# A last product's operand loads placed behind w3's loads, five of its sums moved from GpSimd to VectorE, and a new order table

## The chip, the cores and the metric

The kernel runs on one core of a Trainium2 chip. The metric is the device time of one execution in microseconds (us); lower is better. The core has TensorE (PE, matrix products), VectorE (DVE), ScalarE (ACT), GpSimd (POOL) and SyncE (SP, which here issues the DMAs).

## The reference

Three stages follow each other, all in fp32. Each of 4608 tokens has 512 features.

```python
# 1. attention, 8 batches x 8 heads, 576 queries, head size 64
k_p = k.reshape(B, H, 72, 8, D).mean(axis=3)      # keys and values pooled by 8
v_p = v.reshape(B, H, 72, 8, D).mean(axis=3)
x = softmax(q @ k_p.T / 8) @ v_p
# 2. first MoE: 512 -> 1024 -> 512
h = x @ w_in
s = h * softmax(h)
x = ((s - mean(s)) / sqrt(var(s) + 1e-6) * g_ln) @ w_out
# 3. second MoE: 512 -> 1024 -> 1024 -> 512
out = ((x @ w1) * (x @ w2)) @ w3 @ w_out
```

## The kernel before, in words

**Precision.** Each fp32 operand of a product is split into a high part, written by ACT (L218), and a low part, source minus high part, written by DVE (L219). A product is three matrix products on PE: high x high, low x high, high x low.

**Stages.** The record has three stages. Up to about 335 us attention runs batch by batch, and the first MoE on the tokens of earlier batches runs beside it. `pr` are normalised probabilities (POOL, L660 and L667), `pt` and `px` their transposes on PE (L685, L688), `kp` pooled keys (DVE, L475), `kv` the loaded keys or values (the sum over pooled values is POOL's, L429), `lt` and `lnl` a transpose of the first MoE's hidden rows on PE (L835) and its low part on DVE (L839), `gwh` and `gwl` the parts of the first MoE's output weights (ACT L377, DVE L378, from `cvb` of L374), `x` the first MoE's output (L849 to L851). Beside this, w1, w2 and others are converted in the background by ACT, DVE and POOL (L291 to L306) and written to device memory (L396).

From there to about 935 us PE forms `p`, the products of the second MoE with w1 and w2 by a seven-product (Strassen-Winograd) scheme (L1154 to L1156). DVE, ACT and POOL combine them into `a`, the elementwise product of both halves, which goes to device memory as `pd` (L1147).

In the last stage w3 and w_out are first multiplied with each other. `load_w3` (L1304) loads one piece of w3, 128x512, into a staging tile `stg` (4 buffers) by four DMAs; `w3_split` writes its parts to one of two alternating pairs of tiles `th0` and `th6`, and `wf_rows` (L1323 to L1325) needs two pieces for each of eight row blocks n. A block is 24 matmuls of 128x512 into `ow`. `upper` and `lower` (L1340 to L1357) form the seven combinations `wf`, `t1` to `t4` of the blocks and split them into `wch`/`wcl` and other `th` tiles. Then `Last` multiplies `pd` with these: for each of nine column groups j, `load` brings two tiles `raw` of 1 MB (4 buffers), `sum` forms s1 to s4 from them on POOL (128x1024, L1386), `split` writes ten rotating operand tiles `bk` (their low part by L219), and `product` runs seven products of 24 matmuls each into `o` (L1402 to L1404). L1434 to L1449 combine these on DVE, and the results are stored.

**Order.** The program is traced in one order and then put into another: ISSUE_ORDER holds for each engine a row of numbers in run-length form, and `issue_order` (L114) chains the engine's instructions in the order that these numbers give. An engine executes its own list in order. It waits for other engines' results by semaphores. Names below carry the loop numbers: `raw0_1` is tile 1 of j = 0, `stg_10164` the staging tile with that number, `lnl2` belongs to unit 2.

Of the kernel before, what the change touches and what calls it, by code (L numbers as in the profile page):

```python
# [24 lines left out]
    ),  # L25
    "Activation": (
# [20 lines left out]
    ),  # L47
    "DVE": (
# [32 lines left out]
    ),  # L81
    "Pool": (
# [9 lines left out]
    ),  # L92
# [38 lines left out]
def attention_moe_kernel(  # L131
# [25 lines left out]
    nc = tc.nc  # L157
# [1203 lines left out]
    FACTORS = ("x11", "s2", "s1", "x12", "s3", "x22", "s4")  # L1361
    free = list(range(10))

    class Last:
# [12 lines left out]
        def sum(self, name):  # L1377
            x = self.x
# [181 lines left out]
```

## Time and profile before

| what | value |
|---|---|
| time, median of 3 runs | 1173.01 us (1172.94 to 1174.21) |
| the profiled execution's own time | 1171.81 us |
| its span in the trace | 1170.0 us |
| mean granted TensorE clock | 0.993 of full speed |
| PE busy | 1133.1 us, 97% |
| DVE, ACT, POOL busy | 937.6, 543.4, 527.1 us |

The time is what the device needs for one execution; the span goes from the first to the last thing that the trace records, and 1.81 us lie outside it. Busy time of an engine is the sum of its instructions without their overlaps. A granted clock of 1.00 is 2.4 GHz on TensorE, 0.50 is 1.2 GHz.

### The profile page before, as it was taken

To read this page: it belongs to the slowest core of one execution; us is meant where nothing else is said; L and a number is where in the kernel's file an instruction comes from. 1 tells how busy PE (TensorE), PEld (TensorE's weight loads), DVE (VectorE), ACT (ScalarE), POOL (GpSimd) and SP (SyncE) were. 2 spreads that over 40 slices of the span, in tenths; PEclk is the share of its full clock that TensorE was granted. 3 is DMA by queue.
4 is the path that set the end of the run, shared out by engine and by line. 5 is a ranking of instruction groups with operands and counts; after the bars stand their busy time and mean duration, and the time that the engine had idled before them with its cause. 6 is when DMAs were issued, how large, how long until landed. Compare 5 with 4: busy or idle time off the path is not lost. (4 is left out here: it accounts for less than half of the span.)

```text
span 1170.0 us, 20192 instructions
## 1 busy us (share of the span) xinstructions
PE 1133.1 (97%) x7146; PEld 1017.6 (87%) x7146; DVE 937.6 (80%) x1392; ACT 543.4 (46%) x1399; POOL 527.1 (45%) x482
## 2 busy tenths in 40 slices
PE   6898999999999999999999999999999989999998
PEld 5688888999999899999998888888888868999998
DVE  6899879989676765596668969989886679999982
ACT  5665657575656565664523113131130155454542
POOL 3554645555332321100056757676763254656520
PEclk9999989999999999999999999999999999999999
DMA  9775576979474722356254624544522264353511
GB/s 255 161 137 151 134 191 196 232 220 235 131 177 125 182 91 90 127 191 204 84 159 131 208 89 163 176 147 162 181 99 108 85 222 136 109 196 131 177 39 73
DMA packets 174117, 178.55 MB, mean 153 GB/s; under 512 B 83392, under 2 KB 116160, under 8 KB 174016
## 3 DMA queue, kind: packets, MB, share of 16 engines
q1 hardware_dynamic: 174016, 177.27, 51.8%
q8 instruction: 56, 0.92, 0.3%
q14 instruction: 45, 0.37, 0.1%
HBM read 114.30 MB, written 62.91 MB: 151 GB/s over the span
## 5 line engine op out<-in xcount | busy, mean ns | idle before, releaser
L849 PE MATMUL x<-lnh,gwh 128*128 128x256 f32 x576 | 164.9, 286 | 0.5 <-ACT gwh L377 0.5
L851 PE MATMUL x<-lnh,gwl 128*128 128x256 f32 x576 | 161.9, 281 | 0.6 <-DVE gwl L378 0.4
L850 PE MATMUL x<-lnl,gwh 128*128 128x256 f32 x576 | 161.7, 281 | 0.0
L849 PEld LDWEIGHTS x<-lnh,gwh 128*128 128x128 f32 x576 | 109.1, 189 | 1.7 <-ACT gwh L377 0.7
L640 ACT ACTIVATE ea<-sc,mx 128x72 f32<-128x72 f32 x320 | 98.1, 324 | 26.2 <-DVE mx L637 22.1
L851 PEld LDWEIGHTS x<-lnh,gwl 128*128 128x128 f32 x576 | 109.0, 189 | 1.2 <-DVE gwl L378 1.2
L850 PEld LDWEIGHTS x<-lnl,gwh 128*128 128x128 f32 x576 | 109.1, 189 | 0.9
L660 POOL TENSOR_TENSOR pr<-ea,sm 128x512 f32<-128x512 f32 x40 | 41.7, 1044 | 139.1 <-DVE sm L656 79.4
L755 PE MATMUL h<-winh,xh 128*128 128x512 f32 x288 | 95.4, 411 | 0.0
L1158 ACT ACTIVATE p<-p 128x512 f32<-128x512 f32 (+1 forms) x40 | 22.1, 551 | 156.2 <-PE p L1156 118.9
L1170 POOL TENSOR_TENSOR a<-a,b 128x512 f32<-128x512 f32 (+1 forms) x40 | 53.2, 1329 | 91.3 <-issue 54.5
L755 PE MATMUL h<-winl,xh 128*128 128x512 f32 x288 | 90.8, 395 | 0.0
L755 PE MATMUL h<-winh,xl 128*128 128x512 f32 x288 | 90.0, 394 | 0.0
L640 ACT ACTIVATION_READ_ACCUMULATOR ea<-sc,mx 128x1 f32 x320 | 67.2, 210 | 0.0
L764 ACT ACTIVATE e<-h,ST 128x1024 f32<-128x1024 f32 x36 | 40.2, 1116 | 56.4 <-DVE ST L763 56.2
L755 PEld LDWEIGHTS h<-winl,xh 128*128 128x128 f32 x288 | 54.3, 189 | 11.9
L755 PEld LDWEIGHTS h<-winh,xl 128*128 128x128 f32 x288 | 54.1, 189 | 11.8
L1154 PE MATMUL p<-th,w1h 128*128 128x512 f32 (+1 forms) x160 | 59.0, 369 | 1.9 <-DVE a L1164 1.9
L1155 PE MATMUL p<-th,w1h 128*128 128x512 f32 (+1 forms) x160 | 58.9, 368 | 0.0
L1156 PE MATMUL p<-th,w1l 128*128 128x512 f32 (+1 forms) x160 | 58.8, 368 | 0.0
L1174 POOL TENSOR_TENSOR a<-a,b 128x512 f32<-128x512 f32 (+1 forms) x40 | 54.0, 1350 | 8.2 <-DVE b L1167 5.8
L770 DVE SCALAR_TENSOR_TENSOR e<-h,e 128x1024 f32<-128x1024 f32 x36 | 44.0, 1221 | 16.4 <-ACT e L764 16.2
(278 smaller groups left out, 3798.1 us busy)
## 6 DMA issues: line engine op xcount, KB each, us to landing
raw<-pd SPq DMA_DIRECT2D x18, 1024.0 KB
pd<-a SPq DMA_DIRECT2D x64, 256.0 KB
ed<-turn SPq DMA_DIRECT2D x28, 512.0 KB
back<-ed SPq DMA_DIRECT2D x112, 128.0 KB
x2d<-xo SPq DMA_DIRECT2D x35, 256.0 KB
kv<-in_k_dram SPq DMA_DIRECT2D x32, 256.0 KB
kv<-in_v_dram SPq DMA_DIRECT2D x32, 256.0 KB
f<-in_moe_w_dram SPq DMA_DIRECT2D x16, 512.0 KB
```

The costliest lines, as they stand in the source:

```text
L640: nc.scalar.activation(e[0:n, x], half[a][:, h], AF.Exp, bias=mx[0:n, x : x + 1], scale=1.0, accum_out=sm[0:n, x : x + 1],)
L660: nc.gpsimd.tensor_tensor(pr[0:n, 0 : H * KM].rearrange("p (h k) -> p h k", h=H), e[0:n, :, 0:KM], s8.to_broadcast([n, H, KM]), ALU.mult,)
L755: nc.tensor.matmul(self.ph[:, a], s_[:, c], w_[:, c, a * 512 : a * 512 + 512], start=first, stop=last)
L770: nc.vector.scalar_tensor_tensor(e, self.hv, -1.0 / F, e, ALU.mult, ALU.mult, accum_out=st[:, 2:3])
L849: nc.tensor.matmul(o, gw[0][:, f, ws], self.th[:, f], start=(f == 0), stop=False)
L850: nc.tensor.matmul(o, gw[0][:, f, ws], self.tl[:, f], start=False, stop=False)
L851: nc.tensor.matmul(o, gw[1][:, f, ws], self.th[:, f], start=False, stop=(f == FC - 1))
L1154: nc.tensor.matmul(o, wh[:, c, fsl], th[:, c], start=c == 0, stop=False)
L1155: nc.tensor.matmul(o, wh[:, c, fsl], tl[:, c], start=False, stop=False)
L1156: nc.tensor.matmul(o, wl[:, c, fsl], th[:, c], start=False, stop=c == 1)
L1170: nc.gpsimd.tensor_tensor(a[:, 0], a[:, 0], b[:, 0], ALU.mult)
L1174: nc.gpsimd.tensor_tensor(a[:, 1], a[:, 1], b[:, 1], ALU.mult)
```

## The change

ISSUE_ORDER gets new rows for all five engines, and the sums of j = 0 (s1, s2, s3, s4) and the first sum of j = 1 (s1) are issued by VectorE instead of GpSimd. No other instruction is added, taken away or given to another engine. Two lines of the table stand for its some 180.

```diff
 ISSUE_ORDER = {
     "PE": (
-        "0:32 5 -6 5:2 -7:4 3:4 4:2 -6:4 2:2 1 -2 1:6 1:4 -5 4:27 7 9 -18:7 1:2 8:2 7:2 -19 9 8:2 -20:6 "
+        "0:32 5 -6 5:2 -7:4 3:4 4:2 -6:4 2:2 1 -2 1:6 1:4 -5 4:22 1 -2 1:3 7 9 -18:7 1:2 8:2 7:2 -19 9 "
...
     FACTORS = ("x11", "s2", "s1", "x12", "s3", "x22", "s4")
+    SUMS_ON_DVE = {(0, f) for f in FACTORS} | {(1, "s1")}
     free = list(range(10))
...
             x[name] = RB.tile([P, 4, U], F32, tag="s", name=f"{name}_{self.j}", bufs=4)
-            nc.gpsimd.tensor_tensor(x[name], x[a], x[b], op)
+            (nc.vector if (self.j, name) in SUMS_ON_DVE else nc.gpsimd).tensor_tensor(x[name], x[a], x[b], op)
```

Line numbers of the change are 2 higher than before up to L1360 and 3 higher from there on, so L1304 is L1306, L1373 is L1376, L1386 is L1389 and L219 is L221.

SP's list, where the first `raw` loads meet w3's loads, before:

```order
L1373 DMA raw0_0_10162<-pd_104 128x4x512
L1373 DMA raw0_1_10209<-pd_104 128x4x512
L1304 DMA stg_10164<-w3f_131 32x4x128 x4
L1373 DMA raw1_0_10321<-pd_104 128x4x512
L1373 DMA raw1_1_10384<-pd_104 128x4x512
L1304 DMA stg_10169<-w3f_131 32x4x128 x4
L1304 DMA stg_10211<-w3f_131 32x4x128 x4
L1304 DMA stg_10216<-w3f_131 32x4x128 x4
L1304 DMA stg_10270<-w3f_131 32x4x128 x4
L1304 DMA stg_10275<-w3f_131 32x4x128 x4
L1373 DMA raw2_0_10474<-pd_104 128x4x512
```

And in the change, the same place, from the load of raw0_0 on:

```order
L1376 DMA raw0_0_10162<-pd_104 128x4x512
L1306 DMA stg_10164<-w3f_131 32x4x128 x4
L1306 DMA stg_10169<-w3f_131 32x4x128 x4
L1306 DMA stg_10211<-w3f_131 32x4x128 x4
L1306 DMA stg_10216<-w3f_131 32x4x128 x4
L1306 DMA stg_10270<-w3f_131 32x4x128 x4
L1376 DMA raw0_1_10209<-pd_104 128x4x512
L1306 DMA stg_10275<-w3f_131 32x4x128 x4
L1306 DMA stg_10323<-w3f_131 32x4x128 x4
L1306 DMA stg_10328<-w3f_131 32x4x128 x4
L1376 DMA raw1_0_10321<-pd_104 128x4x512
L1376 DMA raw1_1_10384<-pd_104 128x4x512
```

raw0_1, raw1_0 and raw1_1 stood ahead of all but the first of w3's remaining pieces, and now the loads of raw1 stand behind all of them; raw0_1 stands behind five pieces instead of none.

DVE's list while the row blocks n = 4 and 5 of w3 times w_out run, before (th0 from stg_10164 and stg_10169 is block 4, th6 from stg_10211 and stg_10216 block 5):

```order
L219 TENSOR_TENSOR wcl_10059<-wf_10203,wch_10058 128x256
L219 TENSOR_TENSOR th0_7021<-stg_10164,th0_7021 128x4x4x32
L219 TENSOR_TENSOR bk1_10053<-raw0_1_10209,bk1_10053 128x1024
L219 TENSOR_TENSOR wcl_10059<-ow5_10225,wch_10058 128x256
L1352 TENSOR_TENSOR t2_10250<-ow5_10225,t1_10207 128x256
L1355 TENSOR_TENSOR t3_10251<-ow5_10225,wf_10203 128x256
L219 TENSOR_TENSOR wcl_10059<-t1_10207,wch_10058 128x256
L219 TENSOR_TENSOR wcl_10059<-t2_10250,wch_10058 128x256
L1357 TENSOR_TENSOR t4_10252<-ow5_10225,t2_10250 128x256
L219 TENSOR_TENSOR bk2_10054<-s2_0_10317,bk2_10054 128x1024
L219 TENSOR_TENSOR th0_7021<-stg_10169,th0_7021 128x4x4x32
L219 TENSOR_TENSOR th3_7024<-t3_10251,th3_7024 128x256
```

And in the change:

```order
L221 TENSOR_TENSOR th0_7021<-stg_10169,th0_7021 128x4x4x32
L221 TENSOR_TENSOR wcl_10059<-wf_10203,wch_10058 128x256
L221 TENSOR_TENSOR wcl_10059<-t1_10207,wch_10058 128x256
L221 TENSOR_TENSOR th6_7027<-stg_10211,th6_7027 128x4x4x32
L221 TENSOR_TENSOR th6_7027<-stg_10216,th6_7027 128x4x4x32
L221 TENSOR_TENSOR wcl_10059<-ow5_10225,wch_10058 128x256
L1354 TENSOR_TENSOR t2_10250<-ow5_10225,t1_10207 128x256
L1357 TENSOR_TENSOR t3_10251<-ow5_10225,wf_10203 128x256
L1389 TENSOR_TENSOR s1_0_10315<-raw0_0_10162,raw0_1_10209 128x1024
L221 TENSOR_TENSOR bk1_10053<-raw0_1_10209,bk1_10053 128x1024
L221 TENSOR_TENSOR th0_7021<-stg_10270,th0_7021 128x4x4x32
L1389 TENSOR_TENSOR s2_0_10317<-s1_0_10315,raw0_0_10162 128x1024
```

The second piece of block 4 stood behind two operand splits `bk` and the work on the block before it (`t2` to `t4` of L1352 to L1357), and now it stands ahead of both. The sum s1 of j = 0 is new on this engine, and so is s2.

DVE's list in the attention stage, around the pooled keys `kp3_1`, before:

```order
L475 TENSOR_REDUCE kp3_0_2047<-kv3_0_1939 128x128
L697 TENSOR_TENSOR ptx4_1729<-px4_0_1735,ptx4_1729 64x128
L637 TENSOR_REDUCE mx4_1_1746<-sc4_1_1_1695 128x4
L696 TENSOR_TENSOR ptl4_1728<-pt4_0_1730,pth4_1727 128x4x128
L297 TENSOR_SCALAR cvb_2127<-cvb_2127 128x512
L475 TENSOR_REDUCE kp3_1_2147<-kv3_1_1979 128x128
L655 TENSOR_SCALAR sm4_1_1747<-sm4_1_1747 128x8
L839 TENSOR_TENSOR lnl2_1790<-lt2_0_0_1791,lnh2_1789 128x4x128
L656 RECIPROCAL sm4_1_1747<-sm4_1_1747 128x8
L839 TENSOR_TENSOR lnl2_1790<-lt2_1_0_1814,lnh2_1789 128x4x128
L839 TENSOR_TENSOR lnl2_1790<-lt2_0_1_1838,lnh2_1789 128x4x128
```

And in the change:

```order
L699 TENSOR_TENSOR ptx4_1729<-px4_0_1735,ptx4_1729 64x128
L477 TENSOR_REDUCE kp3_0_2047<-kv3_0_1939 128x128
L639 TENSOR_REDUCE mx4_1_1746<-sc4_1_1_1695 128x4
L698 TENSOR_TENSOR ptl4_1728<-pt4_0_1730,pth4_1727 128x4x128
L841 TENSOR_TENSOR lnl2_1790<-lt2_0_0_1791,lnh2_1789 128x4x128
L477 TENSOR_REDUCE kp3_1_2147<-kv3_1_1979 128x128
L657 TENSOR_SCALAR sm4_1_1747<-sm4_1_1747 128x8
L658 RECIPROCAL sm4_1_1747<-sm4_1_1747 128x8
L841 TENSOR_TENSOR lnl2_1790<-lt2_1_0_1814,lnh2_1789 128x4x128
L841 TENSOR_TENSOR lnl2_1790<-lt2_0_1_1838,lnh2_1789 128x4x128
```

The first `lnl2` stood behind kp3_1 and a step on `sm4_1`, and now it stands ahead of them; a step of a background conversion (L297) has left this place. In the same way `kp2_0` stands some 15 rows later in the change, behind the steps on L374 and L378 that it preceded, and POOL's sum `kv2_0` (L429) stands behind `pr3_0` and `pr3_1` instead of ahead of them. The loads of kv3 stand earlier on SP: one 512 KB load and one store of conversions that preceded them now follow.

## Rows read from the trace of the kernel before

**Rows 1.** The page: span, and busy time by engine.

```profile
span 1170.0 us, 20192 instructions
...
PE 1133.1 (97%) x7146; PEld 1017.6 (87%) x7146; DVE 937.6 (80%) x1392; ACT 543.4 (46%) x1399; POOL 527.1 (45%) x482
```

**Rows 2.** PE's waits, whole run: total us, times, longest us.

```profile
PE ow L1323 <- ACT th L218: 4.6, 1, 4.6
PE pt L685 <- POOL pr L660: 3.2, 5, 1.1
PE lt L835 <- DVE lnl L839: 2.8, 3, 1.3
...
PE px L688 <- POOL pr L667: 0.8, 1, 0.8
...
PE x L849 <- ACT gwh L377: 0.5, 1, 0.5
PE x L851 <- DVE gwl L378: 0.4, 1, 0.4
```

**Rows 3.** The chain of waits, 930 to 975 us: start, us, what.

```profile
939.59 8.75 DMA raw<-pd
...
949.20 5.98 DMA stg<-w3f
955.20 2.01 DVE th L219
957.21 3.35 DVE bk L219
...
963.81 0.62 ACT th L218
```

**Rows 4.** Timeline of PE, 964 to 972 us: start, us, instruction, [idle before].

```profile
964.47 0.80 PE L1323 MATMUL ow<-o,th 128*128 128x512 f32 x1 [4.63 <-ACT th L218]
...
970.37 0.41 PE L1324 MATMUL ow<-o,th 128*128 128x512 f32 x1
...
971.98 0.39 PE L1325 MATMUL ow<-o,th 128*128 128x512 f32 x1
```

**Rows 5.** Windows: length; PE, PEld, DVE, ACT, POOL busy; granted clock; DMA share; GB/s.

```profile
36.00:40.00 4.00, 2.55 (x8) 0.97 (x6) 3.90 (x9) 1.46 (x5) 1.51 (x2) 1.00 1.08 223
...
140.00:160.00 20.00, 16.66 (x111) 14.40 (x110) 18.04 (x35) 12.25 (x39) 9.38 (x14) 0.95 0.72 171
160.00:180.00 20.00, 20.00 (x125) 18.57 (x124) 14.39 (x22) 8.40 (x30) 12.05 (x15) 0.88 0.67 179
...
155.00:159.00 4.00, 1.40 (x9) 0.90 (x10) 4.00 (x11) 1.98 (x4) 2.60 (x4) 0.87 0.89 192
...
1000.00:1020.00 20.00, 20.00 (x171) 20.00 (x170) 20.00 (x15) 10.37 (x12) 12.35 (x5) 1.00 0.47 159
```

**Rows 6.** Timelines of DVE and POOL around the first sums.

```profile
947.96 1.21 DVE L219 TENSOR_TENSOR bk<-raw,bk 128x1024 fp32r<-128x1024 f32 x1
...
957.13 3.43 DVE L219 TENSOR_TENSOR bk<-raw,bk 128x1024 fp32r<-128x1024 f32 x1
...
956.62 2.86 POOL L1386 TENSOR_TENSOR s<-raw 128x1024 f32<-128x1024 f32 x1
```

**Rows 7.** Timelines of DVE and of PE in the last products.

```profile
990.49 1.22 DVE L219 TENSOR_TENSOR th<-s,th 128x1024 fp32r<-128x1024 f32 x1
...
986.49 0.28 PE L1402 MATMUL o<-wch,bk 128*128 128x256 f32 x1
...
1003.37 0.28 PE L1402 MATMUL o<-th,th 128*128 128x256 f32 x1
```

**Rows 8.** Timelines of DVE and POOL in the attention stage.

```profile
101.83 1.93 DVE L475 TENSOR_REDUCE kp<-kv 128x128 f32<-128x1024 f32 x1
...
153.51 1.97 DVE L475 TENSOR_REDUCE kp<-kv 128x128 f32<-128x1024 f32 x1 [0.50 <-DMA kv<-in_k_dram]
...
108.81 3.34 POOL L429 TENSOR_TENSOR kv<-kv 128x512 f32<-128x512 f32 x3 [3.49 <-DMA kv<-in_v_dram]
```

164 rows, old and new, of the table ISSUE_ORDER are left out of this document.

## The prediction

> **What bounds the kernel now.** I read the page's busy times first. PE works in 1133.1 of 1170.0 us [rows 1], so what can be won is its idle time, 36.9 us, and the stretches in which its clock is halved. What the other engines do costs something only where PE waits for it.
>
> The view of PE's waits says where the idle time is [rows 2]. Apart from the wait for the very first load, which no reordering here touches, the largest single one is 4.6 us, before a matmul of `ow` (w3 times w_out), for a split by ACT. The others are short, up to 1.3 us each, and most of them belong to the attention stage: `pt` and `px` for the probabilities of POOL, `lt` for the low part `lnl` of DVE, `x` for `gwh` and `gwl`.
>
> The chain of waits tells what the 4.6 us are made of [rows 3]. From 939.59 two tiles `raw` land, for 8.75 us, and w3's pieces are in the chain only from 949.20 to 955.18. DVE's split of the first such piece then takes 2.01 us, an operand split `bk` stands behind it with 3.35 us, and ACT's split of the second piece comes last, at 963.81. PE starts at 964.47 after a wait of 4.63 us [rows 4]. So loads of operands that PE first uses at 986.49 [rows 7] stand ahead of data that PE needs now, and on DVE their splits do the same.
>
> The windows give the third loss, the clock. Between 140 and 180 us the granted clock is 0.95 and then 0.88 of full speed [rows 5]. Half speed for a share of 2 x 0.05 and 2 x 0.12 of 20 us each is 6.8 us at 1.2 GHz. Ahead of it PE was busy for only 1.40 of 4.00 us (155 to 159 us). After the wait at w3 the same happens: from 964.47 to 970.37 thirteen matmuls take 5.90 us, 0.454 each, while the seven from 970.37 to 971.98 take 0.230 each [rows 4].
>
> **The change part by part.** *The seam at w3.* In the new SP list eight pieces of w3 stand behind raw0_0, the last three of them behind raw0_1 too. Two tiles and one piece (2.3 MB) took 8.75 us [rows 3], so a tile is about 4 us, and the next piece has been issued some 4 us earlier even if the whole of raw0_0 must land first. On DVE the two pieces of block 4 are split without the 3.35 us of `bk` and the four steps on `t2` to `t4` between them. Before, ACT had the second piece done at 964.43. Taking away 4 us of loading, 3.35 us of `bk` and half of the 2.01 us split beside POOL gives 956, against PE's need at 959.84 (964.47 less 4.63): the wait goes, with 4 us to spare. Later blocks follow at 5.5 us each (24 matmuls of 0.230), while a pair of pieces takes ACT 1.2 us (two of 0.62) and DVE at most 4.0 (two of 2.01), so nothing is late next there. The term is 4.6 us, and as lower bound 3.35 us, the `bk` split alone.
>
> The halved clock behind it goes with the wait. Thirteen matmuls at 0.454 instead of 0.230 are 2.9 us. The two together are 7.5 us. Bounds: 3.35 and 7.5.
>
> *What the held operands cost.* PE starts on j = 0 at 986.49 [rows 7], so raw0_1, issued behind five pieces, has time. Where can lateness come through? The seventh operand of j = 0 is split on DVE until 991.71 and used by PE at 1003.37 [rows 7], 11.7 us of slack, the least of all operands that I compared. PE coming 7.5 us earlier leaves 4.2 us, if DVE does no better than before.
>
> *Five sums on DVE.* A 128x1024 step takes DVE 1.21 us alone; five are 6.1 us. The sums on POOL took 2.9 us [rows 6], five some 14 us. While one ran, DVE's split of the same size took 3.43 instead of 1.21 us, so DVE lost up to 2.2 us for each of them, 11 us in all. I take DVE's account as even to 5 us better; its bound on the other side is 6.1 us worse, if the losses came from the remaining sums of POOL just as well. Then the 4.2 us would be 1.9 us short at that operand, and the start of j = 1 also depends on s1 of j = 1, which now stands late in DVE's list behind the held loads. DVE is full in this stage (20.00 of 20.00 us) [rows 5], so what is late there is not made up quickly. In the forecast this costs nothing.
>
> *Attention.* The new lists move conversions and pooling behind work that PE waits for. I price what the rows show:
> - `kv2_0`'s sum waits 3.49 us on POOL for a load and runs 3.34 us until 112.1, and `pr` comes directly behind [rows 8]. It now stands behind that `pr`. PE's longest wait for `pr` is 1.1 us [rows 2]; it goes.
> - `kp2_0` takes 1.93 us of DVE ahead of the steps for `gwh` and `gwl` [rows 8], and PE waits 0.5 and 0.4 us for these [rows 2]. It now stands behind them: 0.9 us.
> - `kp3_1` waits until 153.51 for its load and takes 1.97 us [rows 8]; the first `lnl2` stands behind it, and PE waits 1.3 us for that [rows 2]. `lnl2` now goes first, so the 1.3 us go, but the probabilities `pr4_1` still stand behind kp3_1, and PE meets that wait instead. kp3's loads stand further ahead on SP, so the 0.5 us for which DVE idles before kp3_1 go, and `lnl2` (half the columns of the 1.21 us split, so about 0.65 us) no longer stands between sm4_1 and its reciprocal; `pr4_1` comes some 1.2 us earlier. Only these 1.2 us of the 2.7 us of waits there (1.3, 0.6 and 0.8) are won.
>
> Sum 3.2 us. Below it lies 0, if steps pushed back make other waits: DVE is busy for 18.04 of 20 us there [rows 5], and what is moved behind one thing stands ahead of another. Above it lie 4.5 us more, the rest of the waits for `pt`, `lt`, `px` and `x` (7.7 us in all) [rows 2].
>
> *The clock at 158 us.* 1.2 us less of idling leaves some 1.4 us of it, and idling of that size (PE busy for 2.55 of 4.00 us from 36 to 40) left the clock at 1.00 [rows 5]. So I take the halved stretch as gone. A clock of 0.87 in the window from 155 to 159 puts its start at 158.0, so it ends at 164.8. PE worked in it from about 159, 5.8 us, half of which, 2.9 us, is won.
>
> The Trainium skill speaks against counting on it. "TensorE: Matmul & The Clock Gate", section "What's actually happening", says that a monitor sets the clock by how busy the array has lately been and that the throttled state is the default, with a transition point that varies. By that rule the remaining idle time can bring the halved clock as before, and the sum would lack the 2.9 us; the trace agrees that idling comes ahead of both stretches.
>
> The sum is 7.5 + 3.2 + 2.9 = 13.6 us. From the profiled execution's 1171.81 us that is 1158.2. That execution lay 1.2 us below the median of the runs, so the forecast for a median is **1159.4 us**.
>
> **The rivals.**
> *Only the seam counts.* The attention lists are reshuffled in many places, and what is won at one wait comes back as another; the clock falls there as before. For it speaks that DVE is nearly full there, and that the 1.3 us at `lnl2` already turn into a later wait in my own account; against it that the named waits have clear causes. 1173.0 - 7.5 = 1165.5 us.
> *The clock alone stays.* Everything goes as in the forecast, but PE still idles 1.5 us before 159 us and the clock is halved. 1159.4 + 2.9 = 1162.3 us.
> *The wait at w3 moves into the last product.* DVE has 6.1 us more and no relief, and the operands of j = 1, whose s1 waits for late loads and DVE, come 2 to 4 us late. 1165.5 + 3 = 1168.5 us without the attention gains. For it: DVE at 20.00 of 20. Against it: 11.7 us of slack.
> *No change.* PE would have to wait at w3 just as long because the load of raw0_0 and a full transfer queue hold the pieces all the same, and nothing is won in attention. The 8.75 us are two tiles, so this needs the second to have been harmless. 1173 us.
> *Slower.* Conversions and pooling gather in the wrong place in attention: DVE has only 2 us in 20 free, so a step of 2 us like kp2_0, put ahead of something that PE waits for, stops PE for as long, and a stop like that at 155 us brings 2.9 us of halved clock with it. Two such places cost 2 x (2.7 + 2.9) = 11.2 us and outweigh the seam; from 7.5 us on it decides the sign. With three (16.8 us): 1173.0 - 7.5 + 16.8 = 1182 us.
>
> **How the numbers follow.** Forecast 0.42, only the seam 0.20, the clock alone 0.15, the wait moved 0.09, no change 0.06, slower 0.08. The forecast's own range is 1155.5 to 1161. For the whole, the low end is the forecast with most of the other short attention waits gone (4 of the 4.5 us): 1155.4, given as 1155.5. The high end takes in the rivals up to the moved wait with a us less than its price: 1167.5. What lies outside is about 0.2. A difference of 0.2%, 2.3 us, is about what can be told from no change here. Faster than that: 0.42 + 0.20 + 0.15 + 0.09 = 0.86; within: 0.06; slower: 0.08.
>
> **What would show it.** In the profile after, PE's wait before `ow` for ACT should be gone, the window from 960 to 980 should have a clock of 1.00, and the first `o` should come 7.5 us sooner after the first `ow`. The waits for `gwh`, `gwl` and the longest for `pr` should be missing, the `lt` wait replaced by a `pt` wait of under 1 us. From 1000 on PE should stay at 20.00 of 20.00; a wait of `o` for a DVE split would show the moved wait. The prediction is wrong if new waits of over 1 us stand in the attention stage, or if the clock is still below 1.00 between 140 and 180 us.

## Result, and the profile after

| kernel | median | runs | ratio to before, 95% interval |
|---|---|---|---|
| before | 1172.97 us (1169.26 to 1174.21) | 4 | |
| change | 1161.48 us (1158.30 to 1162.66) | 4 | 0.9896 [0.9865, 0.9927] |

The change is faster by 11.5 us, 1.0% (0.7 to 1.4%). Measured again in two later groups it had the ratios 0.9906 [0.9892, 0.9921] and 0.9902 [0.9882, 0.9922]. Its profiled execution took 1161.34 us, 10.5 us less than that of before. Three executions, one each of before and of experiments 4 and 9, were far slower at a mean clock of 0.66 to 0.82, and the ratios leave them out.

The page's first lines of the change, to be held against [rows 1]:

```profile
span 1159.6 us, 20174 instructions
...
PE 1129.1 (97%) x7146; PEld 1015.5 (88%) x7146; DVE 925.3 (80%) x1397; ACT 542.9 (47%) x1399; POOL 516.5 (45%) x477
```

PE's waits over the whole run of the change, as in [rows 2] (total us, times, longest):

```profile
PE pt L687 <- POOL pr L662: 3.6, 4, 1.7
...
PE x L852 <- DVE lnl L828: 0.9, 1, 0.9
PE x L851 <- ACT lnh L827: 0.7, 1, 0.7
PE lt L837 <- DVE lnl L841: 0.6, 1, 0.6
...
PE px L690 <- POOL pr L669: 0.4, 1, 0.4
```

The 4.6 us before `ow` are not in the list any more, and neither are the waits for `gwh` and `gwl`. New are two waits of `x` for `lnh` and `lnl`, one of 1.7 us for `pr`, and in the middle stage one of 1.1 us of `p` for `b`.

Windows of the change, with the columns of [rows 5]:

```profile
140.00:160.00 20.00, 19.32 (x140) 17.52 (x139) 18.22 (x33) 13.05 (x39) 13.14 (x16) 1.00 0.91 203
155.00:159.00 4.00, 4.00 (x33) 3.87 (x32) 3.32 (x5) 1.21 (x2) 3.84 (x5) 1.00 0.99 147
160.00:180.00 20.00, 20.00 (x142) 18.71 (x141) 17.41 (x29) 14.73 (x55) 10.13 (x14) 1.00 0.69 210
180.00:200.00 20.00, 18.44 (x95) 15.58 (x94) 16.84 (x35) 12.55 (x47) 9.19 (x15) 0.91 0.76 213
...
960.00:980.00 20.00, 20.00 (x107) 17.23 (x106) 20.00 (x35) 13.37 (x26) 2.40 (x2) 1.00 0.57 183
...
1000.00:1020.00 20.00, 20.00 (x172) 20.00 (x171) 20.00 (x14) 11.30 (x14) 16.11 (x6) 1.00 0.46 156
```

The halved clock of 140 to 180 us has gone, a shorter one stands between 180 and 200, and at w3 PE works through. From the first `ow` matmul to the first `o` matmul it needs 43.5 us (932.49 to 976.01) where before needed 51.7 (934.83 to 986.49 [rows 7]). PE's timeline in the change, then in before:

```profile
932.49 0.39 PE L1325 MATMUL ow<-o,th 128*128 128x512 f32 x1
...
976.01 0.28 PE L1405 MATMUL o<-wch,bk 128*128 128x256 f32 x1
```

```profile
934.83 0.39 PE L1323 MATMUL ow<-o,th 128*128 128x512 f32 x1
```

Where the 10.5 us came from can be followed along PE's stream in these two executions, since its instructions are nearly the same. The second half of unit 2's `x` starts at 178.53 before and at 171.00 after: 7.5 us won in the attention stage. At 211 us 5.5 of them are left, at 280 us 2.9, at the first `ow` 2.3. From the first `o` on it is 10.5.

At w3, the timelines of SP and of DVE in the change:

```profile
936.75 0.41 SPq L1376 DMA_DIRECT2D raw<-pd  x1
937.25 13.98 SPq L1306 DMA_DIRECT2D stg<-w3f  x20
951.33 0.39 SPq L1376 DMA_DIRECT2D raw<-pd  x1
951.81 8.49 SPq L1306 DMA_DIRECT2D stg<-w3f  x12
960.35 11.68 SPq L1376 DMA_DIRECT2D raw<-pd  x3
```

```profile
949.45 0.69 DVE L221 TENSOR_TENSOR th<-stg,th 128x512 fp32r<-128x512 f32 x1
...
958.11 1.23 DVE L1389 TENSOR_TENSOR s<-raw,raw 128x1024 f32<-128x1024 f32 x1 [1.53 <-DMA raw<-pd]
959.25 1.22 DVE L221 TENSOR_TENSOR bk<-raw,bk 128x1024 fp32r<-128x1024 f32 x1
```

The second piece of block 4 is split by 950.14. PE starts the block at 954.25 and needs that piece after twelve matmuls, 2.7 us later, so there are 6.8 us to spare. The split of raw0_1 takes 1.22 us, where the same step took 3.43 us beside a sum of GpSimd [rows 6].

Where the attention stage gave time back, the timelines of DVE and POOL around 267 us in the change:

```profile
265.63 1.99 DVE L477 TENSOR_REDUCE kp<-kv 128x128 f32<-128x1024 f32 x1 [1.96 <-DMA kv<-in_k_dram]
267.54 0.20 DVE L657 TENSOR_SCALAR sm<-sm 128x8 f32<-128x8 f32 x1
```

```profile
266.98 1.67 POOL L431 TENSOR_TENSOR vl<-vl 128x256 f32<-128x256 f32 x3 [8.27 <-DMA vl<-in_v_dram]
...
268.60 1.04 POOL L662 TENSOR_TENSOR pr<-ea,sm 128x512 f32<-128x512 f32 x1
```

Here a pooling step that waits for a load stands ahead of `sm8_1` on DVE and of `pr8_1` on POOL, the same pattern that the change removes for `lnl2` at 153 us. The other place is 187 us: the change has PE start `x` of unit 3 ahead of `av5_0`, and PE waits 0.65 us for `lnh3` and 0.87 us for `lnl3`, whose data has just come back from device memory. The clock falls to half speed behind that for 3.6 us (0.09 of 20 us, twice).

### The profile page after: what moved, and what is told of

Same layout as the page of the kernel before. It is cut to its first block, busy times and chain, and to the rows that moved or that the text cites. A ratio compares the mean times of both kernels' runs of the same rounds, so it can differ in the third digit from the quotient of the medians.

```text
span 1159.6 us, 20174 instructions
## 1 busy us (share of the span) xinstructions
PE 1129.1 (97%) x7146; PEld 1015.5 (88%) x7146; DVE 925.3 (80%) x1397; ACT 542.9 (47%) x1399; POOL 516.5 (45%) x477
```

## Experiments

Each kernel changes the order table, and some the engine of the sums. The diffs name the instructions that move, since the table's numbers tell a reader nothing. Ratios are to before, timed in the same group in rounds; differences in us are worked out from the ratio. The group's medians of before were 1171.26, 1170.52 and 1170.24 us.

**1 and 2. The two halves apart.** Experiment 1 takes the lists of before up to the end of the middle stage and those of the change from there; experiment 2 the other way round.

```diff
 # e1_seam                            # e2_attention
-lists of before from the last p on   -lists of before up to the last p
+lists of the change, sums on VectorE +lists of the change, sums on GpSimd
```

> The new order and the five sums on VectorE from the last PE products with w1 and w2 on (the place where w3 times w_out is formed, and the last product); the attention stage and the middle stage in the order of before. Theory (the two parts are separate and add up): the wait before ow and the halved clock behind it go, 8.1 us less than before, ratio 0.993, PE 20.00 of 20 us from 940 to 1020. Rival (the last product only profits because the attention stage arrives earlier or leaves less work behind): 4 us or less.

> The other half: the new order up to the end of the middle stage, then the order of before with its sums on GpSimd. Theory (separate parts): 2.4 us less than before, as the two traces show at the first matmul of ow; the 4.6 us wait before ow and its halved clock stay as they were. The named waits give 7.5 us up to 180 us, and three new places give 5 back. Rival (the attention lists bring nothing in the mean of several runs, because the halved clock moves about): within 1 us of before.

Measured: e1_seam 1163.33 us, 0.9939 [0.9924, 0.9954], 7.1 us less than before; no wait of PE from 930 us to the end. e2_attention 1168.10 us, 0.9979 [0.9964, 0.9993], 2.5 us less, and before `ow` stands, in PE's waits from 930 us on:

```profile
PE ow L1325 <- ACT th L220: 4.6, 1, 4.6
```

The product of the two ratios is 0.9918, within the interval of the change's own. The halves are separate and add up, and three quarters of the gain lie at w3. The rival of the first fell. That of the second (within 1 us of before) is not excluded: at the upper end of the interval the gain is 0.8 us.

The windows of these profiles say something on the halved clock. From 140 to 180 us, e1_seam, then e9_sums_only (below), both with the attention lists of before:

```profile
140.00:180.00 40.00, 36.20 (x254) 32.87 (x253) 34.95 (x59) 22.86 (x79) 22.39 (x28) 1.00 0.76 192
```

```profile
140.00:180.00 40.00, 37.06 (x238) 33.67 (x239) 32.38 (x57) 20.84 (x71) 21.26 (x27) 0.91 0.71 176
```

Both have the waits of before between 150 and 165 us (1.7 us at `lt`, 1.3 in before; 0.6 at `pt`; 0.8 and 0.3 at `px`). One has the halved clock and one has not.

**3. Loads early.** The change with raw0_1 and both tiles of raw1 where before has them.

```diff
 raw0_0
+raw0_1
 stg_10164 (4 DMAs)
+raw1_0
+raw1_1
 stg_10169, 10211, 10216, 10270
-raw0_1
 stg_10275, 10323, 10328
-raw1_0
-raw1_1
 raw2_0
```

> The change, but raw0_1, raw1_0 and raw1_1 are loaded where before has them, ahead of all but one of the remaining pieces of w3. Theory of the prediction (the early loads are half of the wait): the second piece of block 4 lands about 952.8, its two splits end at 954.2 at the earliest against PE's need at 954.25, and the next pieces follow close, so waits of 1 to 4 us come back in w3 times w_out, and 1162.5 to 1166 us. Rival (the place of the splits on ACT and VectorE alone removes the wait; the loads are hidden anyway): waits under 0.5 us, time as the change.

Measured: 1162.03 us, 0.9931 [0.9916, 0.9946]. `ow` runs through in 43.6 us. In the last product PE's waits from 930 to 1000 us are, and then the ACT timeline at the second piece of block 4:

```profile
PE o L1406 <- DVE wcl L221: 1.7, 2, 1.3
```

```profile
957.08 0.63 ACT L220 ACTIVATE th<-stg 128x512 fp32r<-128x512 f32 x1 [5.44 <-DMA stg<-w3f]
```

The piece does land late, at 957.0 with the first `ow` at 933.74, but its split stands ahead of the operands' and is done just as PE comes to it. So the theory was wrong on `ow`: with the sums on VectorE the loads need not be held for it, the place of the splits is enough. What the held loads bring is elsewhere. With the loads early the splits bunch up behind the late piece, and in this execution the last matmuls of the run stand 2.2 us further from the first `o` (180.4 us instead of 178.2). The ratio is 0.0025 to 0.0035 above the change's three, 3 to 4 us.

**4 and 7. The sums on GpSimd again.** Both are the change with the five sums on GpSimd. In experiment 4 POOL's list is that of before; in 7 each sum stands behind the `t1` steps that it would hold up.

```diff
 # POOL, from the end of the middle stage
 # e4: t1(0) s1_0 t1(2) s2_0 s3_0 s4_0 s1_1 t1(4) s2_1 ...
 # e7: t1(0) t1(2) s1_0 t1(4) s2_0 s3_0 s4_0 t1(6) s1_1 s2_1 ...
-    (nc.vector if (self.j, name) in SUMS_ON_DVE else nc.gpsimd).tensor_tensor(x[name], x[a], x[b], op)
+    nc.gpsimd.tensor_tensor(x[name], x[a], x[b], op)
```

> The change, with the five sums on GpSimd again, in the order that GpSimd had them in before. Theory (a sum on GpSimd costs VectorE 2.2 us by contention, more than the 1.21 us that it takes there): four sums beside the splits of blocks 6 and 7 take 8.8 us from VectorE and free 4.9, so the splits come 3.9 us later against 1.8 us of slack: waits of about 2 us before ow and a time 2 us above the change. Rival (VectorE comes out even): no wait before ow, time within 0.5 us of the change.

> The change with the five sums on GpSimd, but each behind the t1 step that it would hold up: t1 of blocks 0 and 2, s1_0, t1 of block 4, s2_0, s3_0, s4_0, t1 of block 6, s1_1. The first version of this took 18 us more, since s1_0 waited there for raw0_1 ahead of a t1 step that ACT and VectorE wait for. Theory (that place alone made the 18 us, and VectorE loses about as much by a sum beside it as by doing it): within 2 us of the change. Rival (contention of sums and splits makes waits of their own): waits before ow of over 2 us, 1164 us or more.

Experiment 4: 1179.86 us, 1.0077 [1.0062, 1.0091], 9 us above before. It tells nothing of contention, that is of what a sum and a VectorE step cost each other when they overlap. Timelines of POOL and ACT:

```profile
954.96 2.40 POOL L1388 TENSOR_TENSOR s<-raw,raw 128x1024 f32<-128x1024 f32 x1 [16.28 <-DMA stg<-w3f]
957.32 0.74 POOL L1345 TENSOR_TENSOR t<-wf 128x256 f32<-128x256 f32 x1
```

```profile
958.10 0.42 ACT L220 ACTIVATE wch<-t 128x256 fp32r<-128x256 f32 x1 [8.92 <-POOL t L1345]
```

s1_0 waits for the held raw0_1, which is issued only at 949.07 (the profile names a piece of w3, which the sum doesn't read, as what landed last). `t1` stands behind it on POOL, and ACT's list, w3's splits in it, waits 8.92 us for `t1`. A load may be held back only if nothing urgent stands behind its first reader.

Experiment 7 takes that away: 1172.20 us, 1.0007 [0.9995, 1.0019], 11.6 us above the change in its group (1160.61). The rival was right, though not on the place. `ow` waits only 0.28 us, but the last product waits for DVE, and from the first `o` to the last matmul PE needs 189.2 us instead of 178.2: 8.1 us of waits and the halved clock behind them. PE's waits from 975 to 992 us, the window from 980 to 1000, and timelines of POOL and DVE:

```profile
PE o L1405 <- DVE wcl L221: 8.1, 2, 7.8
```

```profile
980.00:1000.00 20.00, 12.15 (x85) 11.95 (x85) 20.00 (x19) 7.28 (x11) 10.52 (x5) 0.74 0.32 105
```

```profile
961.45 2.58 POOL L1388 TENSOR_TENSOR s<-s,raw 128x1024 f32<-128x1024 f32 x1
```

```profile
961.69 2.62 DVE L221 TENSOR_TENSOR wcl<-wf,wch 128x256 fp32r<-128x256 f32 x1
964.23 0.41 DVE L1359 TENSOR_TENSOR t<-ow,t 128x256 f32<-128x256 f32 x1
964.56 2.31 DVE L221 TENSOR_TENSOR th<-t,th 128x256 fp32r<-128x256 f32 x1
966.79 3.42 DVE L221 TENSOR_TENSOR bk<-s,bk 128x1024 fp32r<-128x1024 f32 x1
```

A 128x256 step of 0.41 us takes 2.62 us, and it ends just behind the sum beside it (964.03). The groups of DVE's instructions from 955 to 990 us, experiment 7 and then the change (busy us, mean ns):

```profile
L221 DVE TENSOR_TENSOR bk<-s,bk 128x1024 fp32r<-128x1024 f32 x3 | 8.1, 2685 | 0.0
L221 DVE TENSOR_TENSOR wcl<-t,wch 128x256 fp32r<-128x256 f32 x5 | 4.7, 947 | 0.0
L221 DVE TENSOR_TENSOR th<-t,th 128x256 fp32r<-128x256 f32 x5 | 3.9, 790 | 0.0
...
L221 DVE TENSOR_TENSOR th<-raw,th 128x1024 fp32r<-128x1024 f32 x1 | 3.4, 3356 | 0.0
```

```profile
L221 DVE TENSOR_TENSOR bk<-s,bk 128x1024 fp32r<-128x1024 f32 x3 | 3.6, 1213 | 0.0
...
L221 DVE TENSOR_TENSOR th<-t,th 128x256 fp32r<-128x256 f32 x6 | 2.3, 416 | 0.0
L221 DVE TENSOR_TENSOR wcl<-t,wch 128x256 fp32r<-128x256 f32 x5 | 2.1, 413 | 0.0
```

In these four groups alone DVE loses 11.1 us beside the sums (3 x 1.47, 5 x 0.53, 5 x 0.37, and 2.14 against a split of 1.21), against the 6.1 us that five sums cost it on its own list. (The change is not free of this: its three splits `th<-s` in this stretch, beside the sums left on GpSimd, take 6.9 us, 3.2 more than alone.) From the first `ow` to the last matmul this profile needs 233.4 us and that of before 229.9, so the last stage is longer than before, and what attention won makes up for it.

**8. The splits' order alone.** Loads early as in 3, sums on GpSimd in the order of before.

```diff
 # the change, with
+SP's loads of raw0_1, raw1_0, raw1_1 as in e3_loads_early
+the five sums on GpSimd, POOL's list as in e4_sums_pool
```

> Of the change at w3 only the order of the splits on ACT and VectorE (and of PE, which is the same): the first four tiles raw loaded early as before, sums on GpSimd in the order of before, attention as in the change. Theory (the splits' place removes the wait, loads and sums are second to it): no wait before ow over 1 us, 1161 to 1164 us. Rival (early loads and sums beside the splits are each enough to bring it back): 2 to 5 us of waits before ow and the halved clock, 1165 us or more.

Measured: 1173.34 us, 1.0019 [1.0008, 1.0030]. PE waits 3.2 us before `ow` for DVE and about 5 us in the last product. The theory fell: the new order without the sums' move is slower than the old order. Contention is not all of it. GpSimd's list has a `t` step directly behind s1_1 (974.16 to 977.03), ACT waits 3.70 us for that step, and PE waits for ACT in 3.4 of the 5 us. On DVE's timeline two splits of w3 that take 0.69 us each alone:

```profile
962.62 5.61 DVE L221 TENSOR_TENSOR th<-stg,th 128x512 fp32r<-128x512 f32 x2
```

**9. The sums alone.** Before, with only the five sums on VectorE.

```diff
 # VectorE's list of before
 bk0<-raw0_0
 wcl<-t2_10144
+s1_0, s2_0, s3_0
 ...
 bk2<-s2_0
 th0<-stg_10169
+s4_0
 ...
 th6<-stg_10216
+s1_1
```

> Before, with the five sums on VectorE and nothing else changed: s1_0, s2_0 and s3_0 directly behind the split of t2 of block 0's pair at which raw0_1 has landed, s4_0 behind the split from stg_10169, s1_1 behind that from stg_10216; all lists as before otherwise, loads early. Theory (the order makes the wait, and the late piece and ACT's list hold it): a wait before ow of over 2.5 us stays, at most 3 us less than before. Rival (the sums beside the splits were the cause all along): the wait before ow falls under 1 us, the halved clock behind it goes, 6 to 8 us less than before.

Measured: 1168.24 us, 0.9976 [0.9962, 0.9990], 2.8 us less than before. PE's waits from 928 to 1010 us, and the chain of waits:

```profile
PE ow L1325 <- ACT th L220: 2.4, 1, 2.4
```

```profile
958.27 1.62 DMA stg<-w3f
959.89 1.03 ACT bk L220
960.91 0.53 ACT th L220
```

The theory held on the time (at most 3 us less) and missed its bound on the wait by little (2.43 us against over 2.5): 2.43 of 4.63 us stay, and the halved clock with them (0.91 from 960 to 980). Behind the landing of the piece DVE is not in the chain any more. The piece lands at 959.89, 0.83 us after PE began to wait, and ACT splits an operand of 1.03 us ahead of it.

**6 and 10. Mending what was given back.** The change, with moves at the three places where it gave time back (6) and at two of them (10).

```diff
 # both: VectorE and GpSimd at 267 us
+sm8_1                     +pr8_1 (3)
 kp5_0                      vl5's sum (3)
-sm8_1                     -pr8_1 (3)
 # both: the middle stage's lists of before on ACT, VectorE and SP
 # 6 alone: PE at 187 us
-x2_3_0 (4) av5_0 (3) x2_3_0 (3) av5_1 (3) h4_1
+av5_0 (5) av5_1 (2) h4_1 ... x2_3_0 (7)
```

> The change with the three places mended at which its attention and middle stages gave time back: sm8_1 ahead of kp5_0 on VectorE and pr8_1 ahead of the sum of vl5 on GpSimd; PE's order of before where the change puts x2_3_0 ahead of av5_0; the middle stage's order of before on ACT, VectorE and SP. Theory (the given-back time lies in these three places): the waits of 1.7, 1.5 and 0.4 us, the halved clock at 190 us and 0.6 us in the middle go, 4 us less than the change, ratio to it 0.9965. Rival (a wait mended comes back at the next instruction that needs the same loads): at most 1.5 us less.

> The change with two of the three mended places: sm8_1 and pr8_1 ahead of kp5_0 and the sum of vl5, and the middle stage's order of before; PE's order at x2_3_0 as in the change. The version with all three was 1.6 per mille above the change, since PE then waited 2.2 us for ptl in front of av5_0 and the clock halved there. Theory (that third place alone did the harm): 1 us less than the change by the middle stage (waits of 2.5 instead of 3.5 us before p), up to 1.7 us more by pr8_1. Rival (the places are below what these runs tell): within 1.5 us of the change either way.

Measured: 6 took 1163.43 us, 0.9922 [0.9906, 0.9939], against 0.9906 of the change in its group; 10 took 1158.07 us, 0.9891 [0.9867, 0.9914], against 0.9902. In 6 PE's waits from 180 to 210 us and the window are:

```profile
PE av L726 <- DVE ptl L698: 2.2, 1, 2.2
```

```profile
180.00:200.00 20.00, 17.06 (x75) 13.66 (x74) 13.63 (x28) 11.96 (x46) 7.53 (x13) 0.83 0.60 179
```

PE arrives there 7 us earlier than before did, and with `av5_0` first it waits for `ptl` instead of `lnh3`, longer. So the rival was right for 6: this order of PE doesn't mend that place. What it costs goes with the clock in these runs: four of the six runs had a mean clock of 0.994 or 0.995 and took 1163.35 to 1163.77 us, and the two with 0.999 and 1.000 took 1160.10 and 1159.60. For 10 the difference to the change is below what the runs tell, so there is no version here that is shown to beat it.

**5 and 11. The change again**, as a control in the groups of 6 to 8 and of 9 and 10.

```diff
 # e5_change_again, e11_change_third: no edit
```

> The change itself, beside the other kernels of this group on one chip. The ratio should lie in the interval of its first measurement (0.9865 to 0.9927); the first two experiments, seam 0.9939 and attention 0.9979, make 0.992 together if the parts are separate.

> The change itself once more as the control beside the two others of this group: ratio to before 0.989 to 0.992.

Measured: 1160.61 us, 0.9906 [0.9892, 0.9921], and 1158.88 us, 0.9902 [0.9882, 0.9922].

## Why the prediction was right, and where it was not

The forecast was 1159.4 us in a range from 1155.5 to 1167.5, and 1161.48 was measured: 11.5 us won where 13.6 had been added up. Point by point:

- *The seam, 7.5 us.* Right: 8.1 us in the profile (51.7 to 43.5), 7.1 us (5 to 9) by itself. The wait and the halved clock behind it went together. But of the three causes that the step subtracted (4 us of loading, 3.35 us of `bk`, half of a split beside POOL) the loading is not needed: experiment 3 has no wait before `ow` with the loads early, as long as the sums are on VectorE.
- *Five sums on DVE, "in the forecast this costs nothing".* This is the term that was mis-sized. Its mechanism was right, that a sum on GpSimd takes more from DVE than the sum itself takes there; the price of 2.2 us each stood in the text. What the step missed is that the new order didn't work without it in any of the three versions tried: with the sums left on GpSimd the change would have been no faster than before (experiment 7, 11.6 us; 4 and 8 are slower still). In experiment 7 the place of the loss is the first products, where the moved-wait rival had looked for it, and not `ow`. In the old order the move brings 2.8 us by itself (experiment 9). Another order of GpSimd's list, with which the sums might stay there, was not looked for.
- *What the held operands cost, "nothing".* Right; no operand of the last product came late in the change.
- *Attention, 3.2 us, and the clock at 158 us, 2.9 us.* The waits for `gwh`, `gwl`, the long one for `pr` and that at `lt` went as forecast, and of the 2.7 us around 157 us 0.4 were left, less than the 1.5 that I had allowed. 7.5 us had been won by 178 us, but about 2 of them are the halved clock of that one execution of before: the profile of experiment 1, with the same lists and a clock of 1.00 there, is 2.1 us ahead of it from 232 to 320 us. What failed is the step that set the postponed work at nothing: 5 us came back at 187, 267 and 860 us, so 2.3 us (2.5 in experiment 2) remain of 6.1. The lower bound of the term had named that. By the prediction's own sign, a new wait of over 1 us in the attention stage, this part was wrong in the profiled execution (1.7 us at 267 us). That wait is 0.9, 0.3 and 0 us in the profiles of experiments 2, 5 and 11, which have the same lists there; the two at 187 us stay at 1.4 to 1.5 us together.
- *The clock as a term.* It should not have been one. The halved stretch of before is there in one profile and missing in another with the same lists (experiments 9 and 1), so a single profile can't credit its going to the change. All ten profiles with the change's attention lists have 1.00 from 140 to 180 us, but in some the clock is low elsewhere (0.91 from 180 to 200 us in the first, 0.91 from 40 to 60 in that of experiment 2). The mean clock of the runs tells more: 0.994 in before (56 runs beside the experiments) and again 0.994 in experiment 2 (12 runs), 0.997 in experiment 1 (6), 0.998 in the change (15 in three groups). By an estimate from these, with 1.2 us for each 0.001 of 1170 us, the clock gave back 2.9 us at w3, as forecast there, and between nothing and 1.4 us in the attention stage, where 2.9 had been put.
- *The rivals.* "Only the seam counts" (1165.5) is 4.0 us from the measurement, the forecast 2.1, but its mechanism, what is won at one wait comes back as another, is what happened to part of the gain in attention. "The clock alone stays" (1162.3) is the nearest, 0.8 us away. Its term is borne out by half or more, and not its reason: around 158 us the change has a clock of 1.00. "The wait moves into the last product" is what the change did without the sums' move (experiment 7).

## What to carry to other kernels

Price a step moved between VectorE and GpSimd by what it does to its neighbours on the other engine: a sum of 2.4 us on GpSimd cost VectorE more than doing it there would have, and with the lists tried here that decided whether the new order brought 11 us or none. Ahead of a stage that needs data now, put the consumers' steps first in the engines' lists and only then look at the loads, and before a load is held look what stands behind its first reader (here a step of 0.74 us for which ACT waited 8.92). Follow PE's arrival times along the whole stream before a list of short waits is added up, since work moved out of one wait's way is still work (7.5 us won at 178 us, 2.3 left at 930), and do it in more than one profile: here one halved stretch of the clock in one of them is worth 2 us.

## What the hardware showed unexpectedly

A VectorE step beside a GpSimd sum doesn't run slower in proportion, it waits for that sum to end: 0.41 us became 2.62, with the sum ending at 964.03 and the step at 964.31. Steps with one operand `ow` from the matmul accumulators don't: `t<-ow,t` took 0.41 us at 960.82 in before, beside a sum that ran from 959.43 to 962.76. DVE's and POOL's timelines there:

```profile
960.82 0.41 DVE L1352 TENSOR_TENSOR t<-ow,t 128x256 f32<-128x256 f32 x1
```

```profile
959.43 3.33 POOL L1386 TENSOR_TENSOR s<-raw,s 128x1024 f32<-128x1024 f32 x1
```

The Trainium skill says this in "SBUF — State Buffer", sections "SBUF: two separate sides" and "Who interferes with whom": the two engines share a port pair that one of them holds for its whole instruction, and VectorE needs it for a second operand from SBUF, the memory in which tiles lie. Both traces agree. The sums on GpSimd wait in turn: 2.40 us alone, 3.26 to 3.39 us beside splits in the last product of the change.

The halved clock comes and goes between executions of one program. With identical lists the window from 140 to 180 us had 0.91 in two profiles and 1.00 in a third, and in the change the stretch at 190 us was in the first profile (0.91) and not in the two later ones (1.00, here the first of them):

```profile
180.00:200.00 20.00, 18.41 (x102) 15.43 (x101) 18.39 (x37) 13.88 (x54) 9.43 (x15) 1.00 0.73 216
```

Such a stretch costs some 2 to 3 us by an estimate from the windows, and it is a good part of what runs of one kernel differ by. The runs show that link: beside experiments 5 to 8, the eight runs of before with a mean clock of at most 0.993 had a median of 1172.8 us, the eleven with 0.995 or more 1169.6, and experiment 6 shows the same (above). Why the clock falls in one execution and not in the next stays open.
